# Experts' weights: three chunks change places around the buffer of the last logits

## The chip, the core and the metric

One core of a Trainium2 chip runs the whole program. The metric is the device time of one execution in microseconds (us); less is better. Where a range is given it is that of several executions.

## What is computed

The reference chains three layers over 2304 tokens (4 batches of 576) of width 512:

1. attention with 8 heads of 64 columns: rotary positions on q and k, `softmax(q k^T / 8) v`;
2. a soft mixture of 8 experts with 4 slots each: `logits = x @ phi`; the softmax of the logits over all tokens mixes the tokens into 32 slots; every expert computes `relu(slot @ w1[e]) @ w2[e]` for its four slots; the softmax over the slots mixes the results back into the tokens;
3. a gated layer: `h = x @ w_in`, `g = h * sigmoid(h)`, `g @ w_out`.

`w1` is 8 x 512 x 1024 and `w2` 8 x 1024 x 512 in fp32: 32 MB of experts' weights, which are used once each, for 32 slots.

## The kernel before

**Three stages.** Attention goes over 16 pairs of heads, with 10 groups of scores each (`scores`, L379). After a batch's four pairs its logits are computed (`batch`, L479). The last batch is done in two halves (`half`, L542), the second of which ends attention: logits, exponentials, transposes and slot sums (L832 to L853). Then come the experts: `layer1` (L873) for two groups of four experts, `hidden_t` (L883), `layer2` (L895) for the same two groups, with `slot_t`, `combine_t` and `combine_split` between the steps of the second `layer2` (L989 to L1007). The last stage is the gated layer in blocks of 768 tokens (L1021 to L1170).

**The experts' weights** are cut into 64 chunks of [128, 1024] fp32: 512 KB of HBM, and 4096 bytes on each partition. Chunk m belongs to step i = m // 8 (0 to 3: w1, 4 to 7: w2). `layer1` uses chunks 0 to 31 in order and `layer2` 32 to 63, four chunks (one for each expert of its group) in one step. A matmul of `layer2` has 32 output rows: the expert e of the four takes columns 32e of the array (L900), and an fp32 matmul shows in the trace as two records; a chunk has two matmuls, so four records, and a step sixteen.

**Where they lie.** Chunks 0 to 19 have places of their own in the pools `wa` and `rw` and are loaded during attention. Chunks 20 to 44 lie in the pool `wb` (L860), which is laid over the memory of attention's pools as they stood when attention began; with `reuse_waits: "tile"` (L856) a tile of it waits only for the old tiles that it overlaps. Chunks 45 to 63 take the places of chunks that are used up (`more`, L968; `slot`, L111).

The tiles of `wb` are allocated in the order of the loop at L861, so the n-th tile of that loop is at bytes 4096 n to 4096 n + 4096 of the pool; call it place n. The old pools lie in the order in which they were made (L196 to L201). The bytes ahead of the pool `ops_d` follow from the tiles' shapes: `tab` 4,608; `ops_b` 16,896 (three of 4,864 and `kd` 2,304); `eb` 5,760; `ops_c` 25,216; `e3` 4,608; `es0` 2,304; together 59,392, which is 14.5 places. The first tile of `ops_d` has the tag `sa0_0` and 4,864 bytes; `last_logits` (L550) takes it over when pair 15 is done with it. So last_logits lies in places 14.5 to 15.7. It is written by `expo` and `keep` (L578, L587), and read last by the transposes at L851.

Counted on in the same way, with what was used last in each place:

| place | old tiles there | last used by |
|---|---|---|
| 13 | tiles of `e3`, start of `es15_0` | `sums(15, 0)`, L435 |
| 14 | `es15_0`, last_logits | transposes L851 |
| 15 | last_logits, `sa0_1` | transposes L851 |
| 16 to 18 | `sa0_1`, `kb0`, `qb1` (operands of pair 15) | last scores of pair 15, L398 |
| 19, 20 | `qb1`, exponentials of pair 15 | last product with v, L426 |
| 21, 22 | v, maxima and scratch of pair 15 (`rs`, `r0`, `es15_1`) | `norm2(15, 1)`, L455 |
| 23, 24 | end of `es15_1`, x of the last batch | last slot sums, L600 |

**The order of the loads** is fixed by SyncE's queue. `load_w` (L126) is called for m = 20 to 44 in that order (L863), and the calls of `more()` follow. A DMA on that queue waits for what its own target needs and for the DMA eight before it; whatever stands behind it waits too. Behind the last chunk come the parts of w_out and w_in that the last stage starts with (L979 to L985).

```python
        for i in (*range(NWA + 4, NWA + 17), NW - 1, NW - 2, *range(NWA + 17, NW - 2)):
            slot_w(i)
        for i in range(NWA + 4, NW):
            load_w(i)
```

With NWA = 16 and NW = 45 the first loop gives places 0 to 12 to chunks 20 to 32, place 13 to chunk 44, place 14 to chunk 43, and places 15 to 24 to chunks 33 to 42.

Of the kernel before, what the change touches and what calls it, by code (L numbers as in the profile page):

```python
# [29 lines left out]
NW = 45  # L30
NWA = 16
# [43 lines left out]
def attn_softmoe_mlp_kernel(ctx: ExitStack, tc: tile.TileContext, qk, v, cst, phi, w1, w2, w_in, w_out, out):  # L75
# [38 lines left out]
    def slot_w(m):  # L114
        i, (h, e) = m // 8, divmod(m % 8, 4)
        k = (1, 2)[i // 4]
        s = slot(m)
        n = s - NWA
        if 0 <= n < 4:
            if n % 2 == 0:  # L120
                w_raw[n // 2] = rw.tile([128, 4 * S], F32, tag=f"raw{n // 2}", name=f"w_{m}")
            w_sb[i, h, e] = w_raw[n // 2][:, 1024 * (n % 2):1024 * (n % 2) + 1024].rearrange("p (k f) -> p k f", k=k)
        else:
            w_sb[i, h, e] = w_pool[n < 0].tile([128, k, 1024 // k], F32, tag=f"w{s}", name=f"w_{m}")
# [66 lines left out]
    with tc.manual_schedule():  # L191
        with ExitStack() as t1:
# [617 lines left out]
            for g in range(NG + 2):  # L810
                i = g % 10
# [43 lines left out]
        def pool2(name, bufs, space=None, st=ctx, **kw):  # L855
            kw.update({"reuse_waits": "tile"}, **({"space": space} if space else {}))  # L856
            return st.enter_context(tc.tile_pool(name=name, bufs=bufs, **kw))

        t2 = ctx.enter_context(ExitStack())
        w_pool[0] = pool2("wb", 1, st=t2, side=left)  # L860
        for i in (*range(NWA + 4, NWA + 17), NW - 1, NW - 2, *range(NWA + 17, NW - 2)):  # L861
            slot_w(i)
        for i in range(NWA + 4, NW):  # L863
            load_w(i)
# [350 lines left out]
```

## Time and profile before

| | |
|---|---|
| median of 3 executions | 647.17 us (647.12 to 649.62) |
| the profiled execution | 647.71 us, its span 645.8 us |
| TensorE, matmuls | 597.1 us busy (92%) |
| TensorE, weight loads | 425.1 us (66%) |
| VectorE / ScalarE / GpSimd | 410.1 / 360.6 / 234.0 us |
| moved by DMA | 113.86 MB, mean 176 GB/s |
| experts' chunks | 64 loads of 512 KB, all on SyncE's queue |

Engines are named PE (TensorE's matmuls), PEld (its weight loads), DVE (VectorE), ACT (ScalarE), POOL (GpSimd) and SPq (SyncE's queue). The shares are means over a run whose stages have different limits: a PE that shows busy may be streaming one of four column groups while the others wait for weights. So the rows that count are those of a single stage, and a wait is read from what ended it.

### The profile page before, as it was taken

The page shows a single profiled execution, that of the slowest core. Times are in us where ns is not written, and L with a number is a line of the kernel's source. Part 1 is how long each engine was busy: PE and PEld are TensorE (multiplying, and loading weights), DVE is VectorE, ACT ScalarE, POOL GpSimd, SP SyncE. Part 2 cuts the span into 40 slices and gives each one's busy share as a digit, 9 for nine tenths or more (in the row PEclk, how much of TensorE's full clock was granted, in tenths as well). Part 3 has the DMA queues.
Part 4 walks back from the last instruction along what each step waited for, and adds up shares of the span by engine and source line. Part 5 has one row for each costly group of instructions (what it writes and reads, how often), then busy time and mean ns, then how long its engine had stood idle before and what let it go on. Part 6 is the DMA issues. An engine that isn't in the chain of part 4 may idle for free.

```text
span 645.8 us, 10527 instructions
## 1 busy us (share of the span) xinstructions
PE 597.1 (92%) x3571; PEld 425.1 (66%) x3571; DVE 410.1 (63%) x865; ACT 360.6 (56%) x920; POOL 234.0 (36%) x195
## 2 busy tenths in 40 slices
PE   5767799999999999999999999988899999999997
PEld 2555476676676766767664333666678888888886
DVE  6688578888787978885324242678965454464442
ACT  3455477676776767776644220588665444353342
POOL 6376357765776757874350000022420000000000
PEclk9679899999999999999989999989999999999999
DMA  6886579987789887878950799935401100020002
GB/s 214 207 222 188 164 188 235 267 215 239 249 232 299 245 253 230 253 197 228 354 209 24 275 387 391 361 100 168 160 2 49 50 0 1 2 98 1 0 1 97
DMA packets 43188, 113.86 MB, mean 176 GB/s; under 512 B 4976, under 2 KB 6272, under 8 KB 41344
## 3 DMA queue, kind: packets, MB, share of 16 engines
q1 hardware_dynamic: 42956, 112.87, 57.0%
q8 instruction: 28, 0.46, 0.3%
q10 hardware_dynamic: 180, 0.34, 0.1%
q14 instruction: 24, 0.20, 0.1%
HBM read 78.12 MB, written 7.60 MB: 133 GB/s over the span
## 4 chain that ended last, share of the span: by engine, by line
PE 69%; ACT 12%; DVE 9%; DMA 5%; issue 3%; POOL 0%; ACTq 0%; DVEq 0%; SPq 0%; POOLq 0%
PE ops L1155 9%; PE ops L1157 9%; PE ops L1156 9%; PE u L426 8%; PE psmx L345 5%; PE st L397 4%; PE l L900 3%; PE st L398 3%; PE s L435 3%; ACT e L399 3%; PE s L437 2%; PE hps L1050 2%; PE l L879 2%; PE u L423 2%; ACT raw L279 2%
## 5 line engine op out<-in xcount | busy, mean ns | idle before, releaser
L399 ACT ACTIVATE e<-st 128x288 f32<-128x288 f32 x256 | 104.2, 419 | 28.3 <-PE st L398 25.7
L1155 PE MATMUL ops<-wo_hi,ghi 128*128 128x512 f32 x288 | 113.1, 393 | 0.0
L1157 PE MATMUL ops<-wo_hi,glo 128*128 128x512 f32 x288 | 112.8, 392 | 0.0
L1156 PE MATMUL ops<-wo_lo,ghi 128*128 128x512 f32 x288 | 112.8, 391 | 0.0
L1057 DVE TENSOR_TENSOR hps<-hps,g 128x384 f32<-128x384 f32 x96 | 50.0, 561 | 81.8 <-ACT g L1054 81.5
L1054 ACT ACTIVATE g<-hps 128x384 f32<-128x384 f32 x96 | 42.6, 490 | 82.0 <-PE hps L1050 81.6
L397 PE MATMUL st<-sa,sa 128*128 128x288 f32 x256 | 86.2, 338 | 0.5 <-ACT e L399 0.5
L359 DVE CUSTOM_DVE_ANT_0 relu<-psmx,relu 128x288 f32<-128x288 f32 x144 | 64.5, 450 | 29.8 <-ACT relu L350 22.1
L411 POOL TENSOR_TENSOR es<-e,e 128x576 f32<-128x576 f32 x31 | 46.2, 1491 | 95.9 <-ACT e L399 95.9
L426 PE MATMUL u<-e,v 128*64 128x288 f32 x512 | 78.2, 422 | 0.0
L398 PE MATMUL st<-qb,kb 65*128 65x288 f32 x256 | 76.6, 301 | 0.0
L350 ACT ACTIVATE relu<-psmx 128x288 f32<-128x288 f32 x144 | 60.0, 419 | 10.1 <-PE psmx L345 7.6
L397 PEld LDWEIGHTS st<-sa,sa 128*128 128x128 f32 x256 | 49.3, 193 | 23.5 <-issue 14.6
L1157 PEld LDWEIGHTS ops<-wo_hi,glo 128*128 128x128 f32 x288 | 54.4, 189 | 11.7 <-issue 0.2
L272 POOL TENSOR_TENSOR raw<-raw,tab 128x576 f32<-128x576 f32 x31 | 55.5, 1795 | 16.2 <-DMA sa<-sa 8.2
L1156 PEld LDWEIGHTS ops<-wo_lo,ghi 128*128 128x128 f32 x288 | 54.3, 189 | 10.2 <-POOL wo_lo L1033 0.4
L1155 PEld LDWEIGHTS ops<-wo_hi,ghi 128*128 128x128 f32 x288 | 54.4, 189 | 9.6 <-issue 0.2
L416 POOL TENSOR_TENSOR es<-es,e 128x576 f32<-128x576 f32 x31 | 54.0, 1741 | 6.6 <-ACT e L399 5.1
L426 PEld LDWEIGHTS u<-e,v 128*64 128x64 f32 x512 | 36.4, 139 | 29.7 <-issue 14.7
L345 PE MATMUL psmx<-sa,sa 128*128 128x288 f32 x160 | 48.5, 320 | 8.0 <-DVE mx L359 6.4
L345 PE MATMUL psmx<-kd,sa 128*128 128x288 f32 x160 | 47.9, 316 | 7.0 <-DVE kd L334 4.5
L1063 DVE TENSOR_TENSOR glo<-hps,ghi 128x384 fp32r<-128x384 f32 x96 | 49.6, 552 | 5.3 <-ACT ghi L1060 2.0
(193 smaller groups left out, 1040.8 us busy)
## 6 DMA issues: line engine op xcount, KB each, us to landing
w<-in_w_dram SPq DMA_DIRECT2D x64, 512.0 KB
sa<-raw SPq DMA_DIRECT2D x56, 288.0 KB
raw<-in_qk_dram SPq DMA_DIRECT2D x13, 1152.0 KB
w_out_raw<-in_w_out_dram SPq DMA_DIRECT2D x16, 512.0 KB
w_in_raw<-in_w_in_dram SPq DMA_DIRECT2D x12, 512.0 KB
v<-in_v_dram SPq DMA_DIRECT2D x15, 320.0 KB
qb<-sa SPq DMA_DIRECT2D x16, 288.0 KB
out_dram<-os SPq DMA_DIRECT2D x18, 256.0 KB
```

Source lines behind the costliest of these rows:

```text
L272: eng.tensor_tensor(out=r[:, hd, 1], in0=r[:, hd, 1], in1=c(1), op=ALU.mult)
L345: pe.matmul(t, lhsT=rem_cols(qa, hd, 128) if u == 4 else qa[:, c0:c0 + 128], rhs=k, start=u != 4 or hd == 0, stop=u != 4 or hd == 1)
L350: act.activation(out=r, in_=t, func=ACTF.Relu)
L359: dve.tensor_tensor_reduce(out=r, in0=mxt.pop((p, u, 1)), in1=r, scale=1.0, scalar=-3.0e38, op0=ALU.add, op1=ALU.max, accum_out=mx[p][:, u ...
L397: pe.matmul(st, lhsT=ka[:, c0:c0 + 128], rhs=qa[:, o:o + HS], start=True, stop=False)
L398: pe.matmul(st, lhsT=kb[0:65, c0:c0 + 128], rhs=qb[0:65, S * hd + HS * h:S * hd + HS * h + HS], start=False, stop=True)
L399: act.activation(out=e[:, hd], in_=st, func=ACTF.Exp, scale=0.125)
L416: add(out=es[p, h], in0=es[p, h], in1=e, op=ALU.add)
L426: pe.matmul(u_ps[p, h][64 * hd:64 * hd + 64, :], lhsT=vt[p][:, c, 64 * hd:64 * hd + 64], rhs=e[:, hd], start=False, stop=c == 3, skip_grou ...
L1155: pe.matmul(t, lhsT=a, rhs=wo_hi[k], start=k == 0, stop=False)
L1156: pe.matmul(t, lhsT=a, rhs=wo_lo[k], start=False, stop=False)
L1157: pe.matmul(t, lhsT=b, rhs=wo_hi[k], start=False, stop=k == 15)
```

## The change

The loop that allocates the tiles of `wb` takes one chunk more before it comes to chunks 44 and 43. Nothing else is different: the loads, their order and their sizes, and all instructions are the same.

```diff
-        for i in (*range(NWA + 4, NWA + 17), NW - 1, NW - 2, *range(NWA + 17, NW - 2)):
+        for i in (*range(NWA + 4, NWA + 18), NW - 1, NW - 2, *range(NWA + 18, NW - 2)):
             slot_w(i)
```

| place | chunk before | chunk after |
|---|---|---|
| 0 to 12 | 20 to 32 | 20 to 32 |
| 13 | 44 | 33 |
| 14 | 43 | 44 |
| 15 | 33 | 43 |
| 16 to 24 | 34 to 42 | 34 to 42 |

## Rows read from the trace of the kernel before

**Rows 1.** The page's first line.

```profile
span 645.8 us, 10527 instructions
```

**Rows 2.** Waits of SyncE's queue, 335 to 338 us: total us, times, longest.

```profile
SPq L134 <- PE lt_ps L851: 21.1, 1, 21.1
```

**Rows 3.** Timeline of SyncE's queue, chunk loads: start us, us, instruction, count.

```profile
329.82 7.29 SPq L134 DMA_DIRECT2D w<-in_w_dram  x5
...
358.25 4.07 SPq L134 DMA_DIRECT2D w<-in_w_dram  x8
```

**Rows 4.** Windows: length, busy us by engine, granted clock, DMA share, GB/s.

```profile
333.00:336.00 3.00, 2.96 (x21) 2.03 (x22) 0.69 (x2) 1.44 (x4) 2.29 (x3) 1.00 1.02 410
345.00:348.00 3.00, 3.00 (x23) 1.41 (x23) 1.76 (x4) 1.49 (x5) 0.00 (x0) 1.00 0.00 0
354.00:357.00 3.00, 2.59 (x26) 0.83 (x21) 1.60 (x6) 1.91 (x6) 0.00 (x0) 1.00 0.00 0
360.00:412.00 52.00, 49.97 (x375) 19.17 (x368) 15.77 (x40) 10.70 (x24) 0.61 (x1) 1.00 1.04 391
```

**Rows 5.** Timeline of PE, end of attention, layer 1: start us, us, instruction.

```profile
342.56 0.71 PE L435 MATMUL s<-es,ones 128*64 128x288 f32 x4
...
345.55 0.29 PE L398 MATMUL st<-qb,kb 65*128 65x288 f32 x1
...
350.21 0.71 PE L426 MATMUL u<-e,v 128*64 128x288 f32 x4
...
356.72 1.06 PE L600 MATMUL sps<-x,dh 96*32 96x256 f32 x12 [0.35 <-DVE dh L594]
357.72 0.47 PE L851 MATMUL lt_ps<-cst_sb,last_logits 32*96 32x32 f32 x6
...
359.45 10.51 PE L879 MATMUL l<-w,si 128*32 128x512 f32 x96
```

**Rows 6.** Timeline of DVE, 335 to 354 us.

```profile
335.28 0.47 DVE L448 SCALAR_TENSOR_TENSOR s<-s,r 128x288 f32<-128x288 f32 x1 [5.90 <-ACT r L444]
...
352.26 0.47 DVE L448 SCALAR_TENSOR_TENSOR s<-s,r 128x288 f32<-128x288 f32 x1 [1.05 <-ACT r L444]
...
353.33 0.46 DVE L455 SCALAR_TENSOR_TENSOR xt<-u,rs 128x288 f32<-128x288 f32 x1
```

**Rows 7.** Window of line L900 alone (layer 2): PE, PEld, clock, DMA share, GB/s.

```profile
379.70:384.88 5.18, 5.17 (x48) 1.86 (x49) 1.00 1.06 388
```

**Rows 8.** Timeline of PEld, second layer 2; in brackets idle time before.

```profile
386.59 0.14 PEld L900 LDWEIGHTS l<-w,ht 128*32 128x32 f32 x2 [0.36 <-DMA w<-in_w_dram]
...
387.94 0.14 PEld L900 LDWEIGHTS l<-w,ht 128*32 128x32 f32 x2 [0.36 <-DMA w<-in_w_dram]
...
388.83 0.11 PEld L900 LDWEIGHTS l<-w,ht 128*32 128x32 f32 x1 [0.32 <-issue]
389.78 0.42 PEld L913 LDWEIGHTS otp<-cst_sb,o 128*128 128x128 f32 x4 [0.84 <-issue]
...
391.21 0.15 PEld L900 LDWEIGHTS l<-w,ht 128*32 128x32 f32 x4
...
395.17 0.42 PEld L959 LDWEIGHTS cst<-cst_sb,ch 128*128 128x128 f32 x4 [0.84 <-issue]
...
395.96 0.22 PEld L900 LDWEIGHTS l<-w,ht 128*32 128x32 f32 x4
...
400.59 0.42 PEld L959 LDWEIGHTS cst<-cst_sb,ch 128*128 128x128 f32 x4 [0.84 <-issue]
...
402.49 0.15 PEld L900 LDWEIGHTS l<-w,ht 128*32 128x32 f32 x4
...
404.18 0.14 PEld L900 LDWEIGHTS l<-w,ht 128*32 128x32 f32 x2 [0.36 <-DMA w<-in_w_dram]
```

**Rows 9.** Timeline of ACT where layer 2 ends.

```profile
406.12 0.60 ACT L910 ACTIVATE o<-l 128x512 f32<-128x512 f32 x1 [9.39 <-PE l L900]
406.61 0.67 ACT L148 ACTIVATE hw_first<-w_out_raw 128x512 f32<-128x512 f32 x1
```

## The prediction, made before the changed kernel ran

> **What bounds the kernel now.** I read the waits of SyncE's queue first, since all chunk loads stand in it. One wait towers over the others around the end of attention: a chunk load waits 21.1 us for the transposes at L851 [rows 2]. The queue's timeline says when: after five loads that end at 337.1 us the next is issued only at 358.25 [rows 3], right behind the last readers of last_logits, which end at 357.72 + 0.47 = 358.19 [rows 5]. By the table of places the first load in the queue's order that lies over last_logits is chunk 33, so that is the one held, and all behind it are held with it.
>
> The windows say what the hold costs. The DMA engines run full at 410 GB/s before it, move nothing from 345 to 348 and from 354 to 357, and then run full at 391 GB/s from 360 to 412 [rows 4]. So DMA bandwidth is wasted for most of 20 us just ahead of a stretch that has too little of it. That it has too little is read from TensorE. While chunks are there, 12 chunks (48 records) of layer 2 go through in 5.18 us, 0.43 us a chunk [rows 7]. From 385 us on weight loads wait for chunks, and these come 1.35 us apart (386.59, 387.94) [rows 8], which is the transfer time: 524,288 bytes / 391 GB/s = 1.34 us. The last chunk is waited for up to 404.18 [rows 8], layer 2 hands over to ScalarE at 406.12 [rows 9], and the last stage starts from there.
>
> **The change, part by part.**
>
> *What goes.* Chunk 33 now lies in place 13, over tiles whose last user is L435 (342.56 + 0.71 = 343.27 [rows 5]). It can be issued 15.0 us earlier. The 21.1 us become a wait of about 6.
>
> *What is late next.* The loads behind it keep their places and so meet waits that 33's wait hid: chunks 34 to 36 the last scores, 345.55 + 0.29 = 345.84; chunks 37 and 38 the last product with v, 350.21 + 0.71 = 350.92; 41 and 42 the last slot sums, 356.72 + 1.06 = 357.78 [rows 5]; 39 and 40 the norm on VectorE, 353.33 + 0.46 = 353.79 [rows 6]. At 1.34 us each, 33 is moved from 343.3 to 344.6, 34 to 36 from 345.8 to 349.9, 37 and 38 from 350.9 to 353.6, 39 and 40 from 353.8 to 356.5 (the lead time from issue to first byte is the same before and after and is left out). All eight fit ahead of 41, which starts at 357.78.
>
> *What is added.* Chunks 44 and 43 take over the wait for last_logits, until 358.19. Behind them in the queue stand chunks 45 to 63 and the first parts of w_out and w_in. It holds them for 0.4 us behind 41 and 42, which need 2.7 us to move anyway: nothing. Chunks 43 and 44 themselves are used in the third step of the first layer 2, about 383.
>
> *The DMA stream.* Before, chunk 33 starts it at 358.25; after, 41 does at 357.78. Everything from 41 on comes earlier by 8 x 1.34 + 0.47 = 11.2 us. The waits for used-up places leave no hole: chunk 52 needs chunk 20, used by 359.45 + 10.51 = 369.96 [rows 5], and its turn in the stream is 357.78 + 11 x 1.34 = 372.5; the first part of w_out needs chunk 45, used by 384.9, and its turn is 357.78 + 23 x 1.34 = 388.6.
>
> *What TensorE can use of it.* The first layer 2 and layer 1 had their chunks in time, so nothing changes up to 384.88. Then four steps of four chunks follow, with transposes between them. A step with its chunks at hand starts its last record 3 x 0.43 = 1.29 us after its first (in the window of rows 7 a step is 5.18 / 3 = 1.73 us, four rounds of 0.43), and 0.95 us later the next work on the whole array begins (388.83 to 389.78 [rows 8]): 2.24 us. Against the rows: step 1 from 384.88 to 389.78, 4.90, less 2.24, is 2.66; step 2 from 391.21 to 395.17, 3.96, gives 1.72; step 3 from 395.96 to 400.59, 4.63, gives 2.39; step 4 from 402.49 [rows 8] to 406.12 [rows 9], 3.63, gives 1.39. Sum **8.16 us**. The transposes between stay as they are.
>
> *Check against the stream.* With 8.16 us off, step 4 runs from 394.3; the last chunk comes at 404.18 - 11.2 = 393.0. The part of w_out that ScalarE takes at 406.61 [rows 9] comes 11.2 earlier and is needed 8.16 earlier. So TensorE sets the end of the stage, by a margin of 3.0 us or two chunks.
>
> *The last stage* hangs on that handover and moves with it; its later loads are released by its own work. The granted clock was 1.00, the upper level of 2.4 GHz, in all windows of [rows 4], so it adds no term. Unknown is what the eight early transfers do to the end of attention beside them. Nearest rows: the same VectorE instruction took 0.47 us at 335.28 beside full DMA and 0.47 at 352.26 beside none [rows 6]. I take nothing; the bounds are a small gain or loss of 0.3 us on 16 us of chain, one part in fifty, which two such rows could not show.
>
> *Weighed against the trace.* Rows 7 show 48 records in 5.18 us, although the program gives all four records of one expert, on the same 32 columns, before the next expert's; done in that order a chunk would take 3 x 0.43 = 1.29 us before the next could begin. The Trainium skill (TensorE: Matmul & The Clock Gate, Part 3: Packing small matmuls) states that matmuls are strictly first in, first out, never reordered. By that rule the four steps would be bound by their own order, and the sum would be near 0; by the row it is 8.16.
>
> **The sum.** Own time of the profiled execution 647.71 (span 645.8 [rows 1] and 1.9 around it), less 8.16: 639.55. It stands 0.54 above the median of the runs, so against the median, 647.17 - 8.16 = **639.0 us**.
>
> **The rivals.**
>
> 1. *The queue stops again, after four chunks.* A wait that I read too early (37 and 38 hang on several tiles each) holds the rest until 357.78. Four chunks and 0.47 are 5.8 us; the last chunk would come at 398.4, the stage would stay DMA-bound and end 5.8 earlier: 641.4. For it: three more waits stand in the queue, each on another tile. Against: six early chunks (8.5 us) already pay for the whole 8.16.
> 2. *More than TensorE's share.* If the steps close faster than 2.24 us, the stream is the bound: 11.2 us, 636.0. Against: layer 2's rate comes from 48 records of this trace.
> 3. *Order binds layer 2.* A step takes 4 x 1.29 us whether chunks are there or not; the DMA waits only cover it, and the time stays near 647. The page named above states such an order. Against it: rows 7, and even the second step before took less (3.96) than such a step would (5.16).
> 4. *The change doesn't do what it says.* If the buffer reached into place 13, chunk 33 would wait as before: 647. Against: 59,392 bytes lie ahead of it, and place 13 ends at 57,344.
> 5. *Slower: the early transfers drag on the end of attention.* Place: the chain from 343.3 to 359.45, where PE, ACT and DVE take turns and nothing was moved before. Each per cent of stretch costs 0.16 us; only from 71% on (8.16 + 3.24 = 11.4 us of 16.1) would the run be measurably slower, at 650.4 or more. At a stretch of 75%, 12.1 us, it would be 651.1. Against: the two equal VectorE rows [rows 6].
>
> **How the numbers follow.** A measurement of this kernel can tell about 0.5%, 3.24 us, from no change: faster means under 643.9, slower over 650.4. Forecast 0.74, rival 1 0.11, rival 2 0.05; these three are faster, 0.90. Rivals 3 and 4, 0.06 and 0.02, are the same, 0.08. Rival 5 0.02, slower. The range reaches from rival 2 (636.0) to rival 1 (641.4), and the scatter of the runs (one of three was 2.4 above the others) widens the upper end: 635.9 to 642.6.
>
> **What would show it.** Right: the 21.1 us wait on L851 gone from the queue or down to about half a us; chunk loads issued near 343, 346, 351 and 354; DMA traffic between 345 and 357; no weight load of L900 waiting for a chunk; four steps of about 2.2 us; ScalarE's L910 for the second group near 398; the stretch after it as long as before. Wrong: a new wait of more than 3 us on the queue between 344 and 357 (rival 1), L900 spaced as before with all chunks landed (rival 3), or longer instructions between 343 and 359 (rival 5). A different order of instructions in the last stage would also break the sum, since I take that stage as moved whole.

## The result and the profile after

The changed kernel took 637.58 us, median of four executions (637.01 to 638.26), beside 648.33 us for the kernel before on the same chip (647.12 to 649.62, four executions): a ratio of 0.9834 with a 95% interval of [0.9807, 0.9862]. Two later groups of the same kernel (e5, e11 below) gave 0.9862 [0.9826, 0.9898] and 0.9902 [0.9877, 0.9926]; one execution of e5 was disturbed (3138 us) and is left out of every comparison. By these three medians the change is worth 1.0 to 1.7%. The forecast was 639.0 us, a ratio of 0.987, in a range of 635.9 to 642.6.

The profiled execution took 637.44 us. Its page, first line, against [rows 1]:

```profile
span 635.6 us, 10532 instructions
```

The waits of SyncE's queue between 325 and 400 us, against [rows 2] (total us, times, longest):

```profile
SPq L134 <- PE u L426: 7.2, 2, 3.9
...
SPq L134 <- PE l L879: 6.6, 4, 4.2
SPq L134 <- PE s L435: 5.8, 1, 5.8
SPq L134 <- PE st L398: 5.4, 2, 3.3
SPq L134 <- PE sps L600: 2.8, 1, 2.8
SPq L134 <- DVE s_b L582: 2.2, 1, 2.2
```

The single wait of 21.1 us on the transposes at L851 is gone, and L851 stands in no wait at all: the queue is held by L600 until 355.6, and by the time it has come to chunks 43 and 44, L851 is done. In its place stand short waits on L435, L398, L426, VectorE and L600, as the table of places has them; the 5.8 us on L435 is the "about 6" of the prediction. For places 21 and 22 the queue names L582, the VectorE instruction that follows the norm at L455; the load is issued at 351.62, as L455 ends (351.13 + 0.46 = 351.59). The four waits on L879 are those for places that layer 1 uses up.

Windows of the same trace, against [rows 4] (length, busy us by engine, granted clock, DMA share, GB/s):

```profile
342.00:345.00 3.00, 3.00 (x23) 1.31 (x21) 2.30 (x5) 1.87 (x6) 0.00 (x0) 1.00 0.69 192
345.00:348.00 3.00, 3.00 (x19) 1.35 (x17) 0.00 (x0) 1.40 (x3) 0.00 (x0) 1.00 0.90 335
348.00:351.00 3.00, 3.00 (x35) 1.36 (x34) 1.72 (x6) 1.78 (x6) 0.00 (x0) 1.00 0.74 250
351.00:354.00 3.00, 2.31 (x21) 0.73 (x20) 1.71 (x6) 1.15 (x5) 0.00 (x0) 1.00 1.00 365
354.00:357.00 3.00, 2.39 (x28) 1.57 (x27) 1.86 (x5) 1.13 (x2) 0.00 (x0) 1.00 0.75 275
357.00:399.00 42.00, 40.43 (x355) 16.17 (x358) 14.97 (x40) 9.21 (x20) 0.61 (x1) 1.00 1.04 391
```

Where the DMA engines stood still before, they now move 192 to 365 GB/s. The full stretch behind it runs at the same 391 GB/s but is over at 399, not 412.

The timeline of PE from the end of attention to the end of layer 2, against [rows 5], and then ACT's handover, against [rows 9]:

```profile
340.37 0.71 PE L435 MATMUL s<-es,ones 128*64 128x288 f32 x4
...
355.52 0.47 PE L851 MATMUL lt_ps<-cst_sb,last_logits 32*96 32x32 f32 x6
...
372.18 1.91 PE L900 MATMUL l<-w,ht 128*32 128x512 f32 x8
374.01 0.70 PE L1119 MATMUL warm<-cst_sb 128*128 128x256 f32 x2
374.64 1.92 PE L900 MATMUL l<-w,ht 128*32 128x512 f32 x8
...
377.52 7.14 PE L900 MATMUL l<-w,ht 128*32 128x512 f32 x64
384.59 0.66 PE L913 MATMUL otp<-cst_sb,o 128*128 128x128 f32 x4
...
386.03 1.94 PE L900 MATMUL l<-w,ht 128*32 128x512 f32 x16
...
388.70 1.94 PE L900 MATMUL l<-w,ht 128*32 128x512 f32 x16
390.58 0.86 PE L959 MATMUL cst<-cst_sb,ch 128*128 128x128 f32 x5
...
392.48 1.94 PE L900 MATMUL l<-w,ht 128*32 128x512 f32 x16
```

```profile
394.60 0.60 ACT L910 ACTIVATE o<-l 128x512 f32<-128x512 f32 x1 [5.13 <-PE l L900]
```

Timeline of PEld in the first lone step of four chunks and behind it, against [rows 8]:

```profile
386.03 0.18 PEld L900 LDWEIGHTS l<-w,ht 128*32 128x32 f32 x8
386.49 0.15 PEld L900 LDWEIGHTS l<-w,ht 128*32 128x32 f32 x4 [0.28 <-issue]
386.92 0.15 PEld L900 LDWEIGHTS l<-w,ht 128*32 128x32 f32 x4 [0.28 <-issue]
387.90 0.43 PEld L959 LDWEIGHTS cst<-cst_sb,ch 128*128 128x128 f32 x4 [0.84 <-issue]
```

No weight load of L900 waits for a chunk any more, where nine waits stood before. Three lone steps of four chunks show 1.94 us each on PE. Up to the next work on the whole array two of them take 1.87 us (386.03 to 387.90, and 388.70 to 390.57 by the weight loads); behind the last one comes the handover.

**Where the time came from.** Cut at two points, the first L879 (layer 1 starts) and ACT's second L910 (layer 2 hands over):

| us | before | after | gain |
|---|---|---|---|
| attention, up to the first L879 | 359.45 | 357.26 | 2.19 |
| layer 1 to the handover | 46.67 | 37.34 | 9.33 |
| handover to the end of the span | 239.68 | 241.00 | -1.32 |
| span | 645.8 | 635.6 | 10.2 |

The middle line is the change. The gain in attention, 2.19 us, is there already at L435 (342.56 before, 340.37 after), ahead of the first load that moves, and the rows between L435 and the first L879 take 16.89 us in both traces. So this line is no part of the change; across the twelve usable profiles of this study, whose attention is the same instruction for instruction, the first L879 starts anywhere from 356.88 to 360.45 us. The last line goes with the place of a fall of the granted clock, told at the end; whether the change has a part in it is not shown.

### The profile page after: what moved, and what is told of

The parts are those of the page before. It is cut to its first block, busy times and chain, and to the rows that moved or that the text cites. A ratio compares the mean times of both kernels' runs of the same rounds, so it can differ in the third digit from the quotient of the medians.

```text
span 635.6 us, 10532 instructions
## 1 busy us (share of the span) xinstructions
PE 587.3 (92%) x3571; PEld 422.0 (66%) x3571; DVE 411.7 (65%) x865; ACT 360.4 (57%) x920; POOL 233.8 (37%) x195
## 4 chain that ended last, share of the span: by engine, by line
PE 67%; ACT 11%; DVE 10%; issue 8%; DMA 3%; POOL 1%; ACTq 0%; DVEq 0%; SPq 0%; POOLq 0%
PE ops L1157 8%; PE ops L1156 8%; PE ops L1155 8%; PE u L426 8%; PE psmx L345 5%; PE st L397 4%; PE st L398 3%; PE s L435 3%; ACT e L399 2%; PE s L437 2%; PE l L900 2%; PE l L879 2%; PE u L423 2%; DMA sa<-raw 2%; PE hps L1050 2%
## 5 line engine op out<-in xcount | busy, mean ns | idle before, releaser
L426 PE MATMUL u<-e,v 128*64 128x288 f32 x512 | 78.1, 422 | 0.0
L398 PE MATMUL st<-qb,kb 65*128 65x288 f32 x256 | 76.5, 300 | 0.0
L426 PEld LDWEIGHTS u<-e,v 128*64 128x64 f32 x512 | 36.1, 138 | 29.6 <-issue 14.4
```

The source lines that it names most:

```text
L398: pe.matmul(st, lhsT=kb[0:65, c0:c0 + 128], rhs=qb[0:65, S * hd + HS * h:S * hd + HS * h + HS], start=False, stop=True)
L426: pe.matmul(u_ps[p, h][64 * hd:64 * hd + 64, :], lhsT=vt[p][:, c, 64 * hd:64 * hd + 64], rhs=e[:, hd], start=False, stop=c == 3, skip_grou ...
```

## The experiments

The reading under test: each chunk that the queue can move before last_logits comes free shortens the DMA-bound stretch by one transfer, 1.34 us, until TensorE's own work in the four steps of the second layer 2 is the bound. The rivals are the prediction's (order binds, the stream binds, something else in the new layout does it). Each edit is of the loop at L861 in the changed kernel unless it is said otherwise; "stage" is the time from the first L879 to ACT's second L910.

**e1, e2, e3: hold the queue again, one, three and five chunks later than before.** The place over last_logits goes to chunk K = 34, 36 or 38.

```diff
-        for i in (*range(NWA + 4, NWA + 18), NW - 1, NW - 2, *range(NWA + 18, NW - 2)):
+        for i in (*range(20, 34), K, 44, *(m for m in range(34, 44) if m != K)):
```

> Chunk 34 takes place 14 over last_logits, chunk 33 keeps place 13; 43 and 44 move away. Theory (the time is the length of the DMA stream behind the held load, 1.34 us a chunk, up to the point where TensorE binds): one chunk ahead of the hold, 1.3 us faster than before, queue wait on L851 of about 11 to 12 us on the load of chunk 34, L900 still waits for chunks. Rival (it is enough that one load gets out of the way, or the gain lies elsewhere than in the number of early chunks): as fast as the change itself, 9 to 10 us faster than before.

> Chunk 36 takes place 14 over last_logits. Theory: three chunks (33 to 35) ahead of the hold, 3 x 1.34 = 4.0 us faster than before; from the first weight load of layer 1 to the handover to ScalarE 46.7 - 4.0 = 42.7 us. Rival: 9 to 10 us faster.

> Chunk 38 takes place 14 over last_logits. Theory: five chunks (33 to 37) ahead of the hold, 5 x 1.34 = 6.7 us faster than before; layer 1 to handover 40.0 us; L900 still waits for chunks, in its last steps only. Rival: 9 to 10 us faster.

**e4: hold it two chunks earlier than before**, at chunk 31.

```diff
-        for i in (*range(NWA + 4, NWA + 18), NW - 1, NW - 2, *range(NWA + 18, NW - 2)):
+        for i in (*range(20, 31), 32, 33, 44, 31, 43, *range(34, 43)):
```

> Chunk 31 takes place 14 over last_logits, so the hold comes two chunks earlier than before. Theory: 2 x 1.34 = 2.7 us slower than before, layer 1 to handover 49.4 us. Rival (the hold of before is only a matter of what lies behind chunk 33): no difference to before.

Measured, with the waits of the weight loads of L900 for chunks (total us, times) as a third witness:

| kernel | chunks moved early | ratio [95%] | wait on L851 | stage | gain | L900 waits for chunks |
|---|---|---|---|---|---|---|
| e4 | -2 | 1.0037 [1.0012, 1.0062] | 26.7 | 48.96 | -2.29 | 3.8, 13 |
| before | 0 | 1 | 21.1 | 46.67 | | 2.8, 9 |
| e1 | 1 | 0.9988 [0.9970, 1.0006] | 14.5 | 45.27 | 1.40 | 2.6, 9 |
| e2 | 3 | 0.9932 [0.9906, 0.9958] | 11.4 | 42.67 | 4.00 | 1.3, 4 |
| e3 | 5 | 0.9906 [0.9879, 0.9934] | 6.8 | 40.32 | 6.35 | 0.9, 3 |
| after | 8 | 0.9834 [0.9807, 0.9862] | none | 37.34 | 9.33 | none |

One chunk is worth 1.40, three 1.33 each, five 1.27 each; two chunks more behind the wait cost 1.15 each. The transfer time was reckoned at 1.34. So the rival of e1 to e3, the full gain from one load alone, fell. For e1 it is the stage that shows the step of 1.40, since the interval of its ratio holds 1. Two sizes were missed: the wait of e1, expected at 11 to 12 us, was 14.5, and e4 lost 2.29 us instead of 2.7.

The trace also records when each load has landed. In the eight profiles in which L900 waits for the last chunk (before, e1 to e4, e6, e7, e9), the handover starts 1.98 to 1.99 us after that chunk has landed, whatever the length of the stage. The stage is DMA-bound there and pays about one transfer for each chunk that the wait pushes behind it. The time in the queue's wait is no measure of this: from e1 to e2 it falls by 3.1 us and the stage by 2.60, from before to e1 by 6.6 and the stage by 1.40. The layer's steps show the bound moving towards the end. Timeline of PE, e2:

```profile
378.25 7.14 PE L900 MATMUL l<-w,ht 128*32 128x512 f32 x64
386.76 3.00 PE L900 MATMUL l<-w,ht 128*32 128x512 f32 x16
390.49 4.71 PE L900 MATMUL l<-w,ht 128*32 128x512 f32 x16
397.04 3.58 PE L900 MATMUL l<-w,ht 128*32 128x512 f32 x16
```

and e3:

```profile
379.16 7.14 PE L900 MATMUL l<-w,ht 128*32 128x512 f32 x64
387.67 1.95 PE L900 MATMUL l<-w,ht 128*32 128x512 f32 x16
390.34 3.42 PE L900 MATMUL l<-w,ht 128*32 128x512 f32 x16
395.59 3.59 PE L900 MATMUL l<-w,ht 128*32 128x512 f32 x16
```

With three chunks the first of the four steps is at TensorE's pace (it ends the 64 records in 7.14 us), with five the second as well (1.95), and only with eight all of them.

**e8: no chunk over last_logits at all.** Places 14 and 15 stay empty, chunks 43 and 44 go behind the others. (All lines below shift by 5: L905 is L900, L915 is L910.)

```diff
+        holes = []
-        for i in (*range(NWA + 4, NWA + 18), NW - 1, NW - 2, *range(NWA + 18, NW - 2)):
-            slot_w(i)
+        for i in (*range(20, 34), None, None, *range(34, 45)):
+            if i is None:
+                w_pool[0].tile([128, 1024], F32, tag=f"hole{len(w_sb)}_{len(holes)}", name=f"hole{len(holes)}")
+                holes.append(0)
+            else:
+                slot_w(i)
```

> The changed kernel with two unused tiles in places 14 and 15, so that no chunk lies over last_logits; 43 and 44 move to places 25 and 26, over the end of x and the scratch behind it. Theory (the wait that 44 and 43 took over costs nothing): the wait on L851 is gone from the queue and layer 1 to handover stays at 37.3 us, within 0.3. Rival (the last chunks' wait still holds what stands behind it): 0.4 us or more faster.

Stage 358.05 to 395.39, 37.34 us, the same as after to the hundredth; ratio 0.9866 [0.9828, 0.9904]. That 43 and 44 still lie over last_logits in the changed kernel costs nothing, as the prediction had it.

**e6 and e7: take TensorE's single matmul of L1123 out.** In both kernels `dummy(1)` puts one matmul over the whole array into the first step of layer 2. e6 takes it out of the changed kernel, e7 out of the kernel before.

```diff
-        dummy(1)
```

> The changed kernel without the one warming matmul (128 x 128, L1119) that stands in the middle of layer 2's first step. Theory (TensorE's own work now sets the handover): the step no longer waits for the whole array twice, the first layer 2 ends about 2.2 us earlier, layer 1 to handover 35.1 us. Rival (the DMA stream is the bound again): 0 to 0.5 us.

> The same matmul taken out of the kernel before. Theory (the stream sets the handover there): nothing, layer 1 to handover 46.7 us, under 0.5 us to either side; the 2.2 us turn into waits for chunks. Rival (TensorE's order sets it there too): 2.2 us faster.

e7 held: stage 46.63 us, ratio 1.0007 [0.9979, 1.0036]; where the stage waits for the stream, less work on TensorE is worth nothing. In e6 the first step does get shorter, two halves of 1.91 and 1.92 us that start 2.5 us apart being one block of 1.94 now, and the first layer 2 ends 2.17 us earlier (the 64 records start 377.38 - 359.29 = 18.09 us after the first L879, not 377.52 - 357.26 = 20.26). But the expected 35.1 us was a miss: the stage takes 37.11, 0.23 less, which is the rival's 0 to 0.5. The ratio of e6 is 0.9840 [0.9786, 0.9895], with four executions from 634.48 to 641.01, too wide to tell it from the changed kernel. Timeline of PE, e6:

```profile
374.20 1.94 PE L900 MATMUL l<-w,ht 128*32 128x512 f32 x16
...
377.38 7.14 PE L900 MATMUL l<-w,ht 128*32 128x512 f32 x64
...
388.56 2.38 PE L900 MATMUL l<-w,ht 128*32 128x512 f32 x16
...
392.77 3.59 PE L900 MATMUL l<-w,ht 128*32 128x512 f32 x16
```

The last two steps are drawn out, and PEld says for what:

```profile
393.10 0.25 PEld L900 LDWEIGHTS l<-w,ht 128*32 128x32 f32 x4 [0.18 <-DMA w<-in_w_dram]
...
394.45 0.14 PEld L900 LDWEIGHTS l<-w,ht 128*32 128x32 f32 x2 [0.36 <-DMA w<-in_w_dram]
```

So in e6 the stream sets the end. The last chunk waited for comes 394.45 - 359.29 = 35.16 us after the first L879; in the kernel before it was 404.18 [rows 8] - 359.45 = 44.73, 9.57 us later. That is e6's own stream and not that of the changed kernel, whose profile shows the last chunk issued much earlier. Timeline of SyncE's queue, the last chunk's load, before and after:

```profile
393.36 0.63 SPq L134 DMA_DIRECT2D w<-in_w_dram  x1
```

```profile
379.83 0.64 SPq L134 DMA_DIRECT2D w<-in_w_dram  x1
```

Counted from the first L879 that is 33.91 and 22.57 us, 11.34 us earlier. By the trace's record of the landing it is 44.68 (404.13) and 33.33 us (390.59), 11.35 us earlier. In e6 the chunk landed at 35.12, in e8 at 34.14, in e10 (below) at 33.37. So the same stream scatters by up to 1.8 us between profiles. Part of it lies at its start. Windows from the first L879 on, after

```profile
357.26:360.26 3.00, 3.00 (x29) 0.93 (x32) 1.24 (x7) 0.00 (x0) 0.00 (x0) 1.00 0.95 347
360.26:363.26 3.00, 3.00 (x32) 0.91 (x28) 0.00 (x0) 0.00 (x0) 0.00 (x0) 1.00 1.05 392
```

and in e6

```profile
359.29:362.29 3.00, 3.00 (x29) 0.93 (x32) 1.24 (x7) 0.00 (x0) 0.00 (x0) 1.00 0.89 295
362.29:365.29 3.00, 3.00 (x32) 0.91 (x28) 0.00 (x0) 0.00 (x0) 0.00 (x0) 1.00 1.01 317
```

show that in these first 6 us e6 moves 3 x (295 + 317) = 1836 KB and the changed kernel 3 x (347 + 392) = 2217. The 381 KB are about 1.0 of the 1.8 us. What slowed the stream in e6 is open. With the stream of the changed kernel's profile e6 would have ended at 33.33 + 1.99 = 35.3 us, an estimate near the 35.1 expected.

**e9 and e10: one chunk more out of the way.** Chunk 41, which waits for the last slot sums at L600, goes to memory that attention never used (place 29, behind five unused tiles); e9 without L1123's matmul, e10 with it. (Lines shift by 3: L903 is L900, L913 is L910.)

```diff
-        for i in (*range(NWA + 4, NWA + 18), NW - 1, NW - 2, *range(NWA + 18, NW - 2)):
-            slot_w(i)
+        for i in (*range(20, 34), 44, 43, *range(34, 41), 42):
+            slot_w(i)
+        for i in range(5):
+            w_pool[0].tile([128, 1024], F32, tag=f"hole{i}", name=f"hole{i}")
+        slot_w(41)
```

> The kernel of e6 (no work of L1123), with chunk 41 moved from place 23 to memory that attention never used (place 29), so that it no longer waits for the last slot sums at L600. Theory (in e6 the stream of chunks had become the bound): one chunk, 1.34 us, leaves the stretch behind L600, so the last chunk comes 1.3 us earlier; the time from the first L879 to ACT's L910 falls from 37.1 to 35.8 us or less (35.1 is what TensorE's own steps allow), and no load of L900 waits for a chunk. Rival (TensorE's order of work set e6's end, the short waits for chunks were incidental): it stays at 37.1 us.

> The changed kernel with chunk 41 moved in the same way, the work of L1123 kept. Theory (in the changed kernel TensorE sets the end of layer 2, with the chunks just ahead of it): nothing to gain, 37.3 us from the first L879 to ACT's L910, and the time of the changed kernel, 637.6 us. Rival (the stream already sets it): 36.0 us, and 1.3 us less.

e10 held: stage 358.38 to 395.72, 37.34 us for the third time, ratio 0.9883 [0.9844, 0.9922]. Whether the free place brought the chunks any earlier e10 does not show, since its last chunk landed at 33.37 us and that of the changed kernel at 33.33. What does show that TensorE sets the end of the changed kernel is that no weight load of L900 waits there, and that the stage stays at 37.34 us whether the last chunk lands at 33.33, 33.37 (e10) or 34.14 us (e8). e9 lies between theory and rival: stage 359.13 to 395.48, 36.35 us, 0.76 less than e6 and not 1.3; ratio 0.9847 [0.9814, 0.9881]. Timeline of PE and of PEld, e9:

```profile
388.40 1.94 PE L903 MATMUL l<-w,ht 128*32 128x512 f32 x16
...
392.18 3.26 PE L903 MATMUL l<-w,ht 128*32 128x512 f32 x16
```

```profile
393.54 0.14 PEld L903 LDWEIGHTS l<-w,ht 128*32 128x32 f32 x2 [0.33 <-DMA w<-in_w_dram]
```

The third step is back at 1.94 us and the last still waits for a chunk. The last chunk landed at 34.37 us, 0.75 earlier than in e6, and the stage is 0.76 shorter: in both the stream sets the end. That chunk 41's new place is what brought it earlier is not shown, because e8 and the changed kernel lie 0.81 us apart in this without such a cause. On one chip e9 took 636.23 us (633.32 to 637.04), e10 638.17 (636.29 to 640.15) and the changed kernel, e11, 638.99 (638.95 to 639.93). e9 has the lowest median of the study, but its ratio of 0.9847 lies within the changed kernel's 0.9834 to 0.9902, so that it is faster is not shown.

**e5 and e11: the changed kernel again.** No edit.

> The changed kernel once more, beside the next three on the same chip. Theory: layer 1 to handover 37.3 us again, and 9.3 us (1.4%) faster than before in the median; what its first profile showed beyond that (attention 2.2 us shorter, last stage 1.3 us longer) does not repeat with these signs, since the change touches neither. Rival (attention or last stage are changed by it): attention again near 357.3 us, last stage again near 241.0 us.

> The changed kernel once more, for a second profile. The time from the first L879 to ACT's L910 is 37.3 us again, since layer 2 hangs on TensorE's own steps; if it was lucky in the first profile, it lies between 37.3 and the 38.5 us of the prediction's sum (46.67 - 8.16). Attention before it and the last stage behind it vary between profiles: layer 1 starts between 357 and 361 us, and the last stage takes 239 to 241 us.

e5 gave 0.9862 [0.9826, 0.9898], the 1.4% expected; of its stages nothing is known. e11 gave 0.9902 [0.9877, 0.9926], and as worded its expectation was a miss: the stage took 40.14 us (356.88 to 397.02). Timeline of PE, e11, and its windows:

```profile
356.88 13.31 PE L879 MATMUL l<-w,si 128*32 128x512 f32 x96
```

```profile
355.00:360.00 5.00, 4.74 (x27) 2.25 (x28) 2.16 (x10) 0.00 (x0) 0.00 (x0) 0.58 0.90 299
360.00:365.00 5.00, 5.00 (x40) 1.31 (x36) 0.00 (x0) 0.00 (x0) 0.00 (x0) 0.74 1.04 355
```

The granted clock, 1.00 (2.4 GHz) in layer 1 of the other profiles, is at its lower level (0.50, 1.2 GHz) in each us from 356 to 362; the 96 records take 13.31 us, not 10.51 [rows 5]. That is 2.80 of 40.14, and what is left is 37.34. From the end of these records on, the two profiles of the changed kernel take the same time: 394.60 - 367.77 = 26.83 and 397.02 - 370.19 = 26.83. In the 5 us up to 355 PE had been busy for 3.97; in the first profile of the changed kernel it was as busy in the same stretch (3.97 from 350.38 to 355.38) and the clock stayed at 1.00, so what made it fall is open. Of what e5 and e11 expected elsewhere, attention was short again (356.88), a little outside the 357 to 361 of e11, and the last stage took 240.2 us, neither the 239.7 of before nor the 241.0 of the first profile.

## Why the prediction was right, step by step

**What goes, what is late next, what is added: held.** The queue's wait of 21.1 us is gone, and the waits that take over are the ones named; for L455 the queue gives its successor L582, though the load goes as L455 ends. L851 was to hold chunks 43 and 44 for up to half a us; it holds nothing, and e8 shows that the overlap costs nothing.

**The stream: held.** One transfer per chunk is shown by e1 to e4 (1.15 to 1.40 us against 1.34). The 11.2 us for eight chunks and the earlier start were 11.35 in the changed kernel's own profile. The prediction had no term for the scatter of the stream: 11.3 in e10, 10.5 in e8.

**What TensorE can use of it: right in kind, 1.17 us too short.** The term that was mis-sized is "2.24 us" for a step with its chunks at hand, worked out as 3 x 0.43 + 0.95. It takes 1.87 us: of the 16 weight loads of such a step eight start at once and four more each 0.43 to 0.46 us later (386.03, 386.49, 386.92), so the last weight loads start 0.89 us after the first, not 1.29, and 0.98 us later comes the next work on the whole array (387.90). There are four rounds of matmuls, as rows 7 had it, but the weights of the last round are loaded one round ahead of it. The 0.95 had been counted from a weight load (388.83 in rows 8), so the sum took that round twice. The gains by step were 3.00, 2.09, 2.76 and 1.51 us (10.07 us from 379.71 to 389.78 before, less 384.59 - 377.52 = 7.07; 3.96 and 4.63 less 1.87; 3.63 less 392.48 to 394.60, 2.12), against 2.66, 1.72, 2.39 and 1.39. Their sum is 9.36; the stage gained 9.33, not 8.16.

**The check of the margin: the verdict held, with less room.** TensorE sets the end of the changed kernel, but by 2.0 us in its own profile (the stream offers 11.35 us, TensorE takes 9.33) and not by 3.0; in e8 it is 1.2 (10.54). Nearly all of the difference is the mis-sized step, since TensorE could use more of the lead than was reckoned. One number of that check was wrong in itself: step 4 was to start at 402.49 less the gains of the three steps ahead of it, 6.77, which is 395.7; the 394.3 also takes off the gain of step 4. Rival 2, the stream as the bound, holds only in e6 and e9, where TensorE's single matmul is out.

**The rule weighed against the trace.** The sum rested on matmuls of different column groups overlapping although the program gives four records of one expert in a row. The three lone steps with all chunks at hand now show it: 1.94 us each on PE, where 4 x 1.29 = 5.16 us would be needed in order. The Trainium skill (TensorE: Matmul & The Clock Gate, Part 3: Packing small matmuls) states that matmuls are strictly first in, first out; for records on different column groups this trace does not agree, 64 records in 7.14 us. e6 adds that one matmul over the whole array between them ends the overlap: with it the 16 records of the first step of layer 2 take two halves of 1.91 and 1.92 us with 2.5 us from one start to the next, without it 1.94 us in all. It also shows that the queue does hold the records expert by expert: the eight ahead of that matmul take as long as all sixteen do without it, so they are the four records each of two experts and not two rounds of all four.

**The other rivals.** Rival 1 (the queue stops after four chunks) fell with the windows: 275 to 365 GB/s from 351 to 357. Rival 3 fell with the 1.94 us, rival 4 with the wait on L435, which only place 13 has. Rival 5 fell with the 16.89 us from L435 to the first L879, equal to the hundredth beside 0.69 to 1.00 of DMA share; the term of nothing was right.

**The last stage moves whole: not quite.** It took 1.32 us longer. Of that, 0.82 is there at the last matmul (235.56 us after the handover before, 236.38 after) and goes with a fall of the clock (below); the other 0.5 lies behind it and is not explained. The prediction put the clock at nothing, from windows at 1.00 in the stage before. 9.33 - 1.32 = 8.0 us is what the profile bears out for the two stages, a ratio of 0.988, which lies between the three comparisons (0.9834, 0.9862 and 0.9902). In the two profiles 2.19 us more are attention; how much of the 10.75 us between the first medians is such scatter is not shown. That the forecast lies so near to the median is in part luck: two misses, TensorE's share 1.17 us too small and the last stage 1.32 us longer, cancelled.

## What to carry to other kernels

In an in-order queue, look for the first load that lies over a late buffer: it holds everything behind it, and what it costs is not its wait but one transfer time for each load that could have moved meanwhile, as long as a transfer-bound stretch follows. Give such a place to the loads that are issued last, and then list every wait that the first one hid. Before calling one engine the bound, price both sides from rows of the same situation (a lone step, counted from weight load to weight load); a margin of 3.0 us on paper was 2.0 in one profile and 1.2 in another, since the stream scatters too. To tell which side binds, look at how long after the last landing the stage ends: 1.99 us wherever the stream set the end here, 3.2 us and more where TensorE did.

## What the runs showed of the hardware

**The granted clock fell behind a half-idle stretch in ten profiles of twelve, and the last stage differs with where.** About 20 to 25 us behind the handover PE is busy half the time (2.51 to 2.58 of 5 us in all twelve) while ACT and DVE split the next block. The windows there, before:

```profile
426.12:431.12 5.00, 2.57 (x10) 1.89 (x9) 4.67 (x9) 4.45 (x10) 0.78 (x1) 0.88 0.07 10
431.12:436.12 5.00, 5.00 (x46) 3.58 (x45) 4.95 (x9) 3.23 (x8) 2.06 (x2) 0.78 0.56 200
```

and after:

```profile
414.60:419.60 5.00, 2.51 (x11) 1.60 (x9) 4.61 (x9) 4.67 (x10) 0.72 (x1) 1.00 0.12 25
419.60:424.60 5.00, 4.54 (x27) 3.29 (x30) 4.95 (x9) 3.02 (x6) 2.11 (x2) 0.66 0.53 185
```

The clock lost is nearly the same in both (0.12 + 0.22 and 0.34 of 5 us), but after it falls later. Up to the first L1050 behind the idle stretch the two traces agree (430.06 - 406.12 = 23.94 us and 418.60 - 394.60 = 24.00 behind the handover); at the first L1050 of the block after that, 442.27 and 431.54, the changed kernel is 0.79 us behind. The last stage took 239.7 to 240.2 us in the six profiles with the early fall (before, e1, e2, e4, e7 and e11, where the two windows show 0.86 to 0.95 and 0.71 to 0.80), 241.0 to 241.1 in the four with the late one (after, e6, e8, e10: 1.00 and 0.66), and 239.2 and 239.4 in e3 and e9, where both windows stay at 1.00. What decides it is open. All four late falls are in kernels with eight chunks or more moved early, but e9 and e11 are such kernels too; so that the change has no part in it is not shown.

**Equal code, unequal times.** Attention, the same instructions in all twelve profiles, ended at 356.9 to 360.5 us, and in e11 layer 1 lost 2.80 us to the clock. A stage cut out between two named instructions repeated to the hundredth (37.34 us in after, e8 and e10) while medians of the changed kernel, taken on three chips, differed by 1.4 us.
